# Attention with a relative-position bias and two MLPs on one core: building the bias table with one operand per row, and finishing the last accumulators in turn

## Chip, cores, metric

One core of a Trainium2 chip. The metric is the device time of one execution in microseconds (us). Before the change it is 931.96 us, the median of three runs (929.51 to 933.3).

## The reference

Three stages follow each other. Attention with 4 batches, 8 heads, 576 positions and head size 64 has a bias that depends on the two positions and the head, not on the batch:

```python
psi_rel = np.log1p(np.abs(rel))                    # rel = i - j
psi_i = np.log1p(np.maximum(pos[:, None], 1.0))
x = (psi_rel / psi_i)[..., None]
h = np.maximum(x @ w1 + b1, 0.0)                   # 32 hidden units
bias = h @ w2                                      # [i, j, head]
scores = q @ k.T / sqrt(D) + bias
attn = exp(scores - max) / (sum + 1e-9);  out = attn @ v
```

Two MLPs over 2304 tokens follow: 512 to 1024 to 512 with a softmax gate and a layer norm, then 512 to 2048 to 512 with a piecewise quadratic. All tensors are float32.

## The kernel before

**Bias table (lines 109 to 291).** The table is built once, in DRAM (`bias_d`), and later read back as windows. Its unit of work is u, 16 query positions by all 8 heads; there are 36 units. Partitions hold 4 positions by 32 hidden units, so a unit has four parts c. `emit_r(u)` makes the rows `r[:, c]`: the row `xr` (log of the distance, the same in all partitions) times a column of `sc1` (w1 over psi_i), then a maximum with `kc[:, 0:1]` (minus b1). So a VectorE instruction has two operands that are columns, one value per partition. ScalarE makes c = 0 in four units of five (`on_act`), VectorE the rest. A row has n = `span(u)` = max(576 - 16u, 16u + 16) entries, 304 to 576, since only the distance counts. `emit_c(u)` multiplies them with `w2b` on TensorE into `o` (four column groups of 32). ScalarE then copies `o` twice into `ow`: the left half of the row reversed (line 285) and the right half (line 286), 591 values together, adding a constant `k0`. SyncE's queue writes `ow` to `bias_d` (line 291).

The loop at line 362 emits `emit_r` of one unit and `emit_c` of the unit before. The order of the units is the list `rbs` (line 125), which goes from both ends: 0, 17, 1, 16, 2, 8, and so on. Windows `bt` of the table (`load_bias`, n = 0 to 8; n is two heads by a block of 128 positions, n = 8 the last 64 positions) are loaded as soon as their units are written: n = 8 in round 12, 0 and 1 in round 17, 4 and 5 in round 27, 2 and 3 in round 33; 6 and 7 come behind the loop, and their units are the last ones written. Every fourth round also does one step of `prep_all` (the split of q and k into two parts).

**Attention.** Steps k = 0, 1, ... take one window each: four TensorE matmuls (line 415), one VectorE instruction that adds the bias and takes the maximum (`e`, line 421), ScalarE's exponential (line 436), transposes and the product with v. Weights are split beside it in `step(bw)`.

**Second MLP (lines 891 to 1123).** It runs in five legs of (token half, hidden slices). Each round has seven TensorE groups in the order `SEQ`; between them `GAPS` sets the products with `wo` of the round before. These add to six accumulators `acc` (128 tokens by 512 each). A block (11, 22, 12 or 21) has three units q, one accumulator each; accumulators 0 to 2 take blocks 11 and 21, accumulators 3 to 5 blocks 22 and 12. At a leg's end `evac` copies an accumulator into `ob` (4 buffers) and stores it; in the last two legs it adds a partial sum `pt` that is loaded from `part_d` (3 buffers: three loads ahead, then one more behind each `evac`). `step(bw)` is VectorE work on late weights.

Buffers are handed out in program order, and each engine and DMA queue works strictly in the order in which its instructions are written.

Of the kernel before, what the change touches and what calls it, by code (L numbers as in the profile page):

```python
# [24 lines left out]
KD = DM // 128  # L25
# [13 lines left out]
def tile_attention_moe_moe(  # L39
# [69 lines left out]
    x1 = wa0.tile([2, S], F32, name="x1")  # L109
    one2 = wa0.tile([2, 128], F32, name="one2")  # L110
    xr = wa0.tile([128, S], F32, name="xr")
    sc1 = wa0.tile([128, S // 4], F32, name="sc1")
# [4 lines left out]
    kc = wa0.tile([128, 32], F32, name="kc")  # L117
# [4 lines left out]

    rbs = [0, 17, 1, 16, 2, 8, 3, 9, 4, 10, 5, 11, 6, 12, 7, 13, 14, 15]
# [5 lines left out]
    wz = ps0.tile([128, 512], F32, name="wz")  # L131
# [4 lines left out]
    nc.vector.memset(one2, 1.0)  # L136
    nc.vector.memset(kc[:, 4:5], 0.0)
# [3 lines left out]
    )  # L141
    nc.vector.tensor_tensor(out=dg[:, 0:32], in0=dg[:, 0:32], in1=sml[:, 0:32], op=ALU.mult)
    nc.vector.tensor_reduce(out=dg[:, 32:33], in_=dg[:, 0:32], axis=AX.X, op=ALU.add)
    nc.vector.tensor_scalar(out=kc[:, 0:1], in0=b1c, scalar1=-1.0, scalar2=None, op0=ALU.mult)
    nc.vector.tensor_copy(kc[:, 5:6], b1c)
# [7 lines left out]
    z = ps0.tile([128, 512], F32, name="zs")  # L153

    for c in range(4):
        nc.tensor.matmul(
            z[32 * c:32 * c + 32, 256:258],
            lhsT=flat(w2b),
            rhs=kc[:, 4:6] if c == 0 else b1c.to_broadcast([128, 2]),
            start=True,  # L160
            stop=True,
        )
    nc.vector.tensor_copy(kc[:, 1:3], z[:, 256:258])
    zx = ps0.tile([128, 2, 512], F32, tag="o", name="zx", bufs=3)

    for a in range(4):
        nc.tensor.matmul(
            z[32 * a:32 * a + 32, 0:S // 4],
            lhsT=one2[:, 0:32],
            rhs=x1.rearrange("p (t a) -> p t a", a=4)[:, :, a],  # L170
            start=True,
            stop=True,
        )
    for hf in range(2):
        nc.tensor.matmul(
            zx[:, hf, 0:HS], lhsT=one2, rhs=x1[:, hf * HS:hf * HS + HS], start=True, stop=True
        )
    for _ in range(8):
        nc.tensor.matmul(wz[:, 0:128], lhsT=wt, rhs=wt, start=True, stop=True)
    nc.scalar.copy(out=halves(xr), in_=zx[:, :, 0:HS])  # L180

    nc.vector.reciprocal(out=sc1, in_=z[:, 0:S // 4])
    nc.vector.memset(sc1[0:32, 0:1], 1.0)
    nc.vector.tensor_scalar(out=sc1, in0=sc1, scalar1=dg[:, 32:33], scalar2=None, op0=ALU.mult)
# [63 lines left out]
    r_t = {}  # L248

# [4 lines left out]
    def on_act(u):  # L254
        return u % 5 != 4

    def emit_r(u):
        n = span(u)
        r = wa0.tile([128, 4, S], F32, tag="r", name="r", bufs=3)
        r_t[u] = r  # L260
        for c in range(4):
            w = sc1[:, 4 * u + c:4 * u + c + 1]
            if c == 0 and on_act(u):
                nc.scalar.activation(out=r[:, c, 0:n], in_=xr[:, 0:n], func=ACTF.Relu, scale=w, bias=b1c)  # L264
            else:
                nc.vector.tensor_scalar(
                    out=r[:, c, 0:n], in0=xr[:, 0:n], scalar1=w, scalar2=kc[:, 0:1], op0=ALU.mult, op1=ALU.max
                )

    def emit_c(u):  # L270
        n = span(u)
# [3 lines left out]
        cuts = [0, n] if n <= 512 else [0, 512, n]  # L275
        o = ps0.tile([128, 2, 512], F32, tag="o", name="o", bufs=3)
        for q, (lo, hi) in enumerate(zip(cuts[:-1], cuts[1:])):
            for c in range(4):
                nc.tensor.matmul(  # L279
                    o[32 * c:32 * c + 32, q, 0:hi - lo], lhsT=flat(w2b), rhs=r[:, c, lo:hi], start=True, stop=True  # L280
                )
        o = flat(o)
        k0 = kc[:, 1:2] if on_act(u) else kc[:, 2:3]
# [105 lines left out]
    def ps_s():  # L389
        return ps.tile([128, 2, 512], F32, tag="s", name="ps_s", bufs=2)  # L390
# [806 lines left out]
```

## Time and profile before

| | us |
|---|---|
| median of three runs | 931.96 |
| profiled execution | 931.13 |
| its span, first to last instruction | 929.4 |
| TensorE busy in it | 902.7 (97%) |
| VectorE busy | 721.0 (78%) |
| ScalarE busy | 608.8 (66%) |
| GpSimd busy | 255.4 (27%) |
| chain that ended last: TensorE, VectorE, ScalarE, DMA | 81%, 7%, 5%, 2% |

Times in rows count from the span's start, and the profiled execution takes 1.7 us beyond its span. Engines: PE is TensorE (PEld its weight load), DVE VectorE, ACT ScalarE, POOL GpSimd, SP SyncE; a q behind the name is that engine's queue. A row's duration can reach into the next instruction's start, so what an instruction costs its engine is the distance from its start to the next start; the text calls this the pitch.

### The profile page before, as it was taken

Reading aid. Unit: us, or ns where it says so; the run is one execution under the profiler, and the core shown is the slowest. Engines: PE = TensorE matmul, PEld = TensorE weight load, DVE = VectorE, ACT = ScalarE, POOL = GpSimd, SP = SyncE. Lnnn points to the kernel's source line nnn. Section 1 sums busy time; section 2 is a strip of 40 time slices with the busy share of each in tenths; the row PEclk is TensorE's granted clock in tenths of the full one; section 3 lists DMA queues with packets and bytes.
Section 4 is the critical chain, followed back from the end, with each engine's and each line's share of the span. In section 5 each row is a group of like instructions: output and inputs, shape, how many; then the busy total and the mean of one; then the engine's idle time right before and its main releaser. Section 6 shows DMA issues by size and latency. Waiting matters only on the chain.

```text
span 929.4 us, 16872 instructions
## 1 busy us (share of the span) xinstructions
PE 902.7 (97%) x6052; PEld 778.2 (84%) x6052; DVE 721.0 (78%) x1540; ACT 608.8 (66%) x1290; POOL 255.4 (27%) x229
## 2 busy tenths in 40 slices
PE   8779999999999999999999999999999999999996
PEld 5138888888889889999999998988898888898885
DVE  7997889898888647888888348888888875576854
ACT  5988989999999857666666633555455444454431
POOL 1015665757575324444366400000000000000000
PEclk9999999999999999999999999999999999999998
DMA  4896373564652101555653678769567865347532
GB/s 143 257 298 197 127 253 132 175 222 134 220 167 90 46 23 60 191 193 193 214 206 137 215 260 302 257 203 318 182 228 253 273 210 164 115 159 248 165 119 102
DMA packets 101351, 173.14 MB, mean 186 GB/s; under 512 B 10450, under 2 KB 65234, under 8 KB 101268
## 3 DMA queue, kind: packets, MB, share of 16 engines
q1 hardware_dynamic: 96000, 165.70, 54.3%
q10 hardware_dynamic: 4900, 4.72, 1.4%
q0 software_dynamic: 368, 1.64, 0.5%
q8 instruction: 48, 0.79, 0.3%
q14 instruction: 35, 0.29, 0.1%
HBM read 125.48 MB, written 46.54 MB: 185 GB/s over the span
## 4 chain that ended last, share of the span: by engine, by line
PE 81%; DVE 7%; ACT 5%; DMA 2%; issue 2%; POOL 1%; SPq 0%; DVEq 0%; ACTq 0%
PE acc L1009 20%; PE ab L970 17%; PE ps_s L415 9%; PE ps_x L512 8%; PE ps_s L558 7%; PE ps_t L480 7%; PE ps_x L836 6%; PE ps_s L836 1%; PE o L279 1%; DMA bias_d<-ow 1%; POOL wp L705 1%; PE ps_t L817 1%; PE ps_t L457 1%; PE ps_t L512 1%; ACT r L264 1%
## 5 line engine op out<-in xcount | busy, mean ns | idle before, releaser
L1009 PE MATMUL acc<-wo,gh 128*128 128x512 f32 x576 | 179.4, 392 | 0.2 <-DVE ob L989 0.2
L421 DVE CUSTOM_DVE_ANT_0 e<-ps_s,bt 128x576 f32<-128x576 f32 x144 | 107.7, 749 | 19.8 <-PE ps_s L415 16.5
L1009 PEld LDWEIGHTS acc<-wo,gh 128*128 128x128 f32 x576 | 105.8, 188 | 15.0 <-DVE ob L989 0.8
L436 ACT ACTIVATE e<-e,su 128x576 f32<-128x576 f32 x144 | 112.7, 782 | 8.6 <-DVE su L421 8.1
L1009 PE MATMUL acc<-wo,gl 128*128 128x512 f32 x288 | 114.3, 397 | 0.0
L415 PE MATMUL ps_s<-kh,sq 128*128 128x288 f32 x320 | 101.3, 334 | 3.2 <-DVE su L421 2.8
L956 ACT CAST gh<-ga 128x384 fp32r<-128x384 f32 x96 | 49.4, 514 | 80.5 <-DVE ga L950 80.5
L481 ACT COPY pt<-ps_t 128x512 f32<-128x512 f32 x144 | 83.7, 582 | 11.7 <-PE ps_t L480 9.9
L415 PE MATMUL ps_s<-kl,sq 128*128 128x288 f32 x320 | 89.9, 298 | 0.0
L970 PE MATMUL ab<-x2d,wr 128*128 128x384 f32 x288 | 84.9, 335 | 1.3 <-DVE cs L941 1.3
L945 ACT ACTIVATE ga<-cs,half_c 128x384 f32<-128x384 f32 x72 | 44.4, 616 | 61.2 <-DVE cs L941 61.2
L480 PE MATMUL ps_t<-ident,e 128*128 128x128 f32 x576 | 84.0, 273 | 0.3 <-ACT pt L481 0.3
L957 DVE TENSOR_TENSOR gl<-ga,gh 128x384 fp32r<-128x384 f32 x96 | 53.1, 553 | 33.5 <-ACT gh L956 33.3
L512 PE MATMUL ps_x<-pt,v 128*64 128x256 f32 x640 | 76.2, 384 | 0.0
L936 ACT COPY pk<-ab 128x384 f32<-128x384 f32 x96 | 45.2, 471 | 47.1 <-PE ab L970 46.9
L836 PE MATMUL ps_x<-lh,woh 128*128 128x256 f32 x256 | 73.4, 287 | 0.1
L836 PE MATMUL ps_x<-lh,wol 128*128 128x256 f32 x256 | 72.1, 282 | 0.0
L836 PE MATMUL ps_x<-ll,woh 128*128 128x256 f32 x256 | 72.1, 282 | 0.0
L941 DVE TENSOR_TENSOR cs<-ab,pk 128x384 f32<-128x384 f32 x72 | 39.8, 553 | 40.9 <-PE ab L970 40.9
L480 PEld LDWEIGHTS ps_t<-ident,e 128*128 128x128 f32 x576 | 69.7, 141 | 1.1 <-ACT pt L481 0.5
L415 PEld LDWEIGHTS ps_s<-kh,sq 128*128 128x128 f32 x320 | 61.0, 191 | 11.1 <-DVE sq L217 5.0
L216 POOL TENSOR_TENSOR kl<-stg,kh 128x576 fp32r<-128x576 f32 (+1 forms) x30 | 47.3, 1578 | 67.7 <-DVE kh L213 62.0
(199 smaller groups left out, 2328.5 us busy)
## 6 DMA issues: line engine op xcount, KB each, us to landing
wr<-wi_d SPq DMA_DIRECT2D x168, 256.0 KB, 3.8
stg<-in_qk_dram SPq DMA_DIRECT2D x30, 640.0 KB, 3.9
raw<-in_w2nd_dram SPq DMA_DIRECT2D x32, 512.0 KB, 3.8
wi_d<-wd SPq DMA_DIRECT2D x24, 512.0 KB, 5.6
bias_d<-ow SPq DMA_DIRECT2D x36, 295.5 KB, 3.9
wo_d<-wd SPq DMA_DIRECT2D x16, 512.0 KB, 3.8
wo<-wo_d SPq DMA_DIRECT2D x16, 512.0 KB, 5.5
st<-x_d SPq DMA_DIRECT2D x16, 384.0 KB, 5.5
```

What stands on the lines that cost most here:

```text
L415: nc.tensor.matmul(sc[:, hf, 0:HS], lhsT=l, rhs=r, start=j == 0, stop=j == len(parts) - 1)
L421: nc.vector.tensor_tensor_reduce(out=halves(e), in0=sc[:, :, 0:HS], in1=halves(b_t[hp, n]), scale=-1.0 / float(D) ** 0.5, scalar=3.0e38, o ...
L436: nc.scalar.activation(out=e, in_=e, func=ACTF.Exp, scale=-1.0, bias=su[:, n:n + 1], accum_out=su[:, 9 + n:10 + n])
L480: nc.tensor.transpose(tp[:, kt * 128:(kt + 1) * 128], e[:, c0:c0 + 128], ident)
L481: nc.scalar.copy(out=pt[:, 4 * h:4 * h + 4, 128 * o:128 * o + 128], in_=tp.rearrange("p (a b) -> p a b", a=4))
L512: nc.tensor.matmul(x[64 * h:64 * h + 64, o0:o0 + w], lhsT=v[:, kt, 64 * h:64 * h + 64], rhs=r, start=kt == 0, stop=kt == 4, skip_group_che ...
L558: nc.tensor.matmul(h[:, hf, :], lhsT=l[:, kk, :], rhs=r[:, kk, c0:c0 + 512], start=kk == 0 and j == 0, stop=kk == KD - 1 and j == 2,)
L836: nc.tensor.matmul(ob[:, a * 256:(a + 1) * 256], lhsT=l, rhs=r[:, f, :], start=f == 0 and j == 0, stop=f == K1 - 1 and j == 2,)
L956: nc.scalar.copy(out=gh, in_=a)
L957: nc.vector.tensor_tensor(out=gl, in0=a, in1=gh.bitcast(F32), op=ALU.subtract)
L970: nc.tensor.matmul(d, lhsT=l, rhs=r[:, kk], start=q in (1, 2, 5) and kk == 0 and m == 0, stop=kk == 1 and m == 2, skip_group_check=True,)
L1009: nc.tensor.matmul(d, lhsT=l, rhs=r, start=first and m == 0, stop=last and m == 2, skip_group_check=True)
```

## The change

The bias is written as (xw + sh) with a maximum against zero, summed over the hidden units with w2, and divided by psi_i only when the product is copied. `xw` is the row times w1, `sh` holds b1 times psi_i. A row instruction now has one column operand and an immediate zero. ScalarE makes c = 3 of every unit with bias alone; VectorE always makes three rows. TensorE writes the whole line of 591 values, reading `r` backwards for the left half, in three pieces of four column groups; ScalarE copies it once, times a column of `rs` (1 / psi_i). `rs` comes from a small load `rc0` (64 by 18 single numbers) that GpSimd rounds, a selection matrix `sel` that GpSimd makes, and two TensorE matmuls. The set-up matmuls use the float32r format.

Units go in rising order, `emit_c` follows two rounds behind with four buffers for `r`, and windows 0 to 5 load in pairs in rounds 13, 21 and 29; 6, 7 and 8 follow behind the loop. Step k = 0 of attention moves into round 35 (its exponential into round 36).

In the second MLP all six `pt` are loaded ahead (6 buffers) and the sum is made in place, `ob` has 3 buffers, the first `step(bw)` moves from round 0, q = 7 to round 1, q = 1, and the last round takes its units in the order of `LAST`.

```diff
+    for hf in range(2):
+        nc.tensor.matmul(zx[:, hf, 0:HS], lhsT=one2, rhs=x1[:, hf * HS:hf * HS + HS], start=True, stop=True)
...
+    nc.scalar.activation(out=halves(xw), in_=zx[:, :, 0:HS], func=ACTF.Copy, scale=dg[:, 32:33])
+    nc.vector.tensor_scalar(out=sh, in0=z[:, 0:S // 4], scalar1=b1c, scalar2=None, op0=ALU.mult)
...
+    def emit_rs():
+        nc.gpsimd.tensor_copy(rc, rc0)
+        nc.gpsimd.tensor_tensor(
+            out=sel.rearrange("p o (g e) -> p (o g) e", e=8),
+            in0=ident[0:64, 0:32].unsqueeze(2).to_broadcast([64, 32, 8]),
+            in1=ident[0:64, 32:64].unsqueeze(2).to_broadcast([64, 32, 8]),
+            op=ALU.add,
+        )
+        for o in range(2):
+            nc.tensor.matmul(
+                z[:, 256 + 32 * o:256 + 32 * o + S // 32], lhsT=sel[:, o], rhs=rc, start=True, stop=True
+            )
+        nc.scalar.copy(out=rs.rearrange("p (t o) -> p o t", o=2), in_=...)
...
-    rbs = [0, 17, 1, 16, 2, 8, 3, 9, 4, 10, 5, 11, 6, 12, 7, 13, 14, 15]
+    rbs = list(range(S // 32))
...
     def emit_r(u):
-            w = sc1[:, 4 * u + c:4 * u + c + 1]
-            if c == 0 and on_act(u):
-                nc.scalar.activation(out=r[:, c, 0:n], in_=xr[:, 0:n], func=ACTF.Relu, scale=w, bias=b1c)
+            w = sh[:, 4 * u + c:4 * u + c + 1]
+            if c == 3:
+                nc.scalar.activation(out=r[:, c, 0:n], in_=xw[:, 0:n], func=ACTF.Relu, bias=w)
             else:
                 nc.vector.tensor_scalar(
-                    out=r[:, c, 0:n], in0=xr[:, 0:n], scalar1=w, scalar2=kc[:, 0:1], op0=ALU.mult, op1=ALU.max
+                    out=r[:, c, 0:n], in0=xw[:, 0:n], scalar1=w, scalar2=0.0, op0=ALU.add, op1=ALU.max
                 )
...
     def emit_c(u):
-        nc.scalar.activation(out=ow[:, 0:M - 1], in_=o[:, 1:M][:, ::-1], func=ACTF.Identity, bias=k0)
-        nc.scalar.activation(out=ow[:, M - 1:M - 1 + F], in_=o[:, 0:F], func=ACTF.Identity, bias=k0)
         w = M - 1 + F
+        for lo, hi in ((0, min(M - 1, 512)), (512, M - 1), (M - 1, max(M - 1, 512)), (max(M - 1, 512), w)):
+            if lo < hi:
+                for c in range(4):
+                    d = r[:, c, M - hi:M - lo][:, ::-1] if lo < M - 1 else r[:, c, lo - M + 1:hi - M + 1]
+                    nc.tensor.matmul(o[32 * c:32 * c + 32, lo:hi], lhsT=flat(w2b), rhs=d, start=True, stop=True)
+        nc.scalar.activation(out=ow[:, 0:w], in_=o[:, 0:w], func=ACTF.Copy, scale=rs[:, u:u + 1])
...
     def evac(g, p, k, d):
-        ob = wc.tile([128, DM], F32, tag="ob", name="ob", bufs=4)
+        ob = part_t.pop(0) if g > 2 else wc.tile([128, DM], F32, tag="ob", name="ob", bufs=3)
         if g > 2:
-            nc.vector.tensor_tensor(out=ob, in0=d, in1=part_t.pop(0), op=ALU.add)
-            load_part(p)
+            nc.vector.tensor_tensor(out=ob, in0=d, in1=ob, op=ALU.add)
...
+    LAST = {
+        1: [(22, 0), (22, 1), (22, 2)],
+        2: [(12, 0), (12, 1), (12, 2)],
+        6: [(11, 0), (21, 0), (11, 1), (21, 1), (11, 2), (21, 2)],
+    }
```

**Order on SP's queue around the end of the table, before.** `bt` is a window (the heads of a pair in one or three pieces), `raw` a piece of the first weights; the last three windows' places are at issue.

```order
L291 DMA bias_d<-ow 16x8x591 x12
L240 DMA bt<-bias_d 64x576 x2
...
L291 DMA bias_d<-ow 16x8x591 x3
L345 DMA raw<-in_win_dram 128x256 x2
L242 DMA bt<-bias_d 128x576
L244 DMA bt<-bias_d 128x512
L245 DMA bt<-bias_d 128x64
L201 DMA v<-in_vp_dram 128x640
```

And with the change:

```order
L299 DMA bias_d<-ow 16x8x591
L258 DMA bt<-bias_d 128x576
L260 DMA bt<-bias_d 128x512
L261 DMA bt<-bias_d 128x64
L299 DMA bias_d<-ow 16x8x591 x8
L353 DMA raw<-in_win_dram 128x256 x2
L258 DMA bt<-bias_d 128x576
L260 DMA bt<-bias_d 128x512
L261 DMA bt<-bias_d 128x64
L256 DMA bt<-bias_d 64x576 x2
L217 DMA v<-in_vp_dram 128x640
```

Window 8 (the piece of 64 positions, twice) moves from the first third of the table to behind windows 6 and 7; what stands between the last write and window 6 is the same.

**Order on ACT at the table's start, before**, from the copy of the row on (`r` a row, `ow` a copied half):

```order
L180 ACTIVATE xr<-zx 128x576
L264 ACTIVATE r<-xr,sml,sc_95 128x576
L264 ACTIVATE r<-xr,sml,sc_95 128x560
L285 ACTIVATE ow<-o,kc 128x15
L286 ACTIVATE ow<-o,kc 128x576
L285 ACTIVATE ow<-o,kc 128x31
L286 ACTIVATE ow<-o,kc 128x560
```

And with the change:

```order
L170 ACTIVATE xw<-zx,dg 128x576
L278 ACTIVATE r<-xw,sh 128x576
L194 COPY rs<-zz 128x2x18
L278 ACTIVATE r<-xw,sh 128x560
L278 ACTIVATE r<-xw,sh 128x544
L295 ACTIVATE ow<-o,rs 128x591
L278 ACTIVATE r<-xw,sh 128x528
L295 ACTIVATE ow<-o,rs 128x591
```

The copy of `rs` stands behind the first row, and every unit has one row and one copy on this engine.

**Order on PE at the very end, before** (accumulators 0 to 5 are 6943, 6944, 6945, 6946, 6949, 6950; gh and gl the two parts of a block; from the fourth unit of the last round on):

```order
L1009 MATMUL acc_6946<-wo_9322,gh 128x512 x2
L1009 MATMUL acc_6946<-wo_9322,gl 128x512
...
L1009 MATMUL acc_6946<-wo_9174,gh 128x512 x2
L1009 MATMUL acc_6946<-wo_9174,gl 128x512
...
L1009 MATMUL acc_6943<-wo_9322,gh 128x512 x2
L1009 MATMUL acc_6943<-wo_9322,gl 128x512
```

And with the change (accumulators 3 and 0 are 7173 and 7170, from the fourth unit of the last round on):

```order
L1019 MATMUL acc_7173<-wo_9401,gh 128x512 x2
L1019 MATMUL acc_7173<-wo_9401,gl 128x512
...
L1019 MATMUL acc_7170<-wo_9401,gh 128x512 x2
L1019 MATMUL acc_7170<-wo_9401,gl 128x512
L1019 MATMUL acc_7170<-wo_9549,gh 128x512 x2
L1019 MATMUL acc_7170<-wo_9549,gl 128x512
```

Block 12 comes three units earlier, and an accumulator of the first three is finished every two units instead of every unit at the very end.

## Rows read from the trace of the kernel before

**Rows 1.** Windows: us, busy us per engine, PE clock, DMA share, GB/s.

```profile
16.00:64.00 48.00, 36.29 (x308) 10.44 (x308) 46.03 (x109) 44.54 (x95) 0.00 (x0) 1.00 0.86 267
80.00:100.00 20.00, 20.00 (x183) 17.10 (x180) 17.26 (x48) 17.20 (x45) 12.89 (x12) 1.00 0.37 116
```

**Rows 2.** Timeline, set-up and first units: start us, us, instruction, idle before.

```profile
1.06 3.78 PE L133 MATMUL wz<-wt 128*128 128x128 f32 x16 [1.06 <-DVE half_c L127]
...
8.98 7.81 DVE L266 TENSOR_SCALAR r<-xr,sc,kc 128x576 f32<-128x576 f32 x16 [1.35 <-ACT xr L180]
...
11.91 3.35 PE L279 MATMUL o<-r,w2b 128*32 128x512 f32 x48
...
14.38 15.12 SPq L291 DMA_DIRECT2D bias_d<-ow  x11
```

**Rows 3.** Groups by form on DVE: busy us, mean ns.

```profile
L266 DVE TENSOR_SCALAR r<-xr,sc,kc 128x576 f32<-128x576 f32 x6 | 3.1, 574 | 1.4 <-ACT xr L180 1.4
...
L266 DVE TENSOR_SCALAR r<-xr,sc,kc 128x304 f32<-128x304 f32 x6 | 2.3, 433 | 0.0
...
L213 DVE CAST kh<-stg 128x576 fp32r<-128x576 f32 x2 | 0.9, 452 | 0.0
...
L184 DVE TENSOR_SCALAR sc<-sc,dg 128x144 f32<-128x144 f32 x1 | 0.3, 296 | 0.0
```

**Rows 4.** Timeline of ACT and DVE, early units, the last rows and the last copy.

```profile
14.57 0.72 ACT L286 ACTIVATE ow<-o,kc 128x560 f32<-128x560 f32 x1
15.18 0.86 ACT L264 ACTIVATE r<-xr,sml,sc 128x576 f32<-128x576 f32 x1
15.94 0.72 ACT L285 ACTIVATE ow<-o,kc 128x559 f32<-128x559 f32 x1
16.55 0.29 ACT L286 ACTIVATE ow<-o,kc 128x32 f32<-128x32 f32 x1
...
60.71 1.45 DVE L266 TENSOR_SCALAR r<-xr,sc,kc 128x512 f32<-128x512 f32 x3
...
63.99 0.32 ACT L286 ACTIVATE ow<-o,kc 128x80 f32<-128x80 f32 x1
```

**Rows 5.** Groups by form on ACT, first 75 us.

```profile
L436 ACT ACTIVATE e<-e,su 128x576 f32<-128x576 f32 x7 | 5.4, 774 | 3.6 <-DVE su L421 3.5
```

**Rows 6.** Chain of waits, table into attention: start us, us, what.

```profile
65.41 4.70 DMA bias_d<-ow
...
70.25 2.81 DMA bt<-bias_d
...
73.19 0.76 DVE e L421
...
74.01 2.29 PE ps_s L415 x8
```

**Rows 7.** Windows behind that wait, columns as in rows 1.

```profile
74.00:76.00 2.00, 1.99 (x8) 1.99 (x9) 1.56 (x5) 2.00 (x5) 0.00 (x0) 0.50 0.98 333
```

**Rows 8.** Timeline of PE, first round of the second MLP.

```profile
551.36 0.45 PE L970 MATMUL ab<-x2d,wr 128*128 128x384 f32 x1 [0.68 <-DVE cs L941]
```

**Rows 9.** Timeline of PE, ACT and DVE at the end.

```profile
915.25 0.62 PE L1009 MATMUL acc<-wo,gh 128*128 128x512 f32 x2
...
921.14 0.39 PE L1009 MATMUL acc<-wo,gl 128*128 128x512 f32 x1
...
915.78 1.22 DVE L957 TENSOR_TENSOR gl<-ga,gh 128x384 fp32r<-128x384 f32 x2
...
921.89 0.69 DVE L989 TENSOR_TENSOR ob<-acc,pt 128x512 f32<-128x512 f32 x1 [1.67 <-DMA out_dram<-ob]
...
925.40 0.69 DVE L989 TENSOR_TENSOR ob<-acc,pt 128x512 f32<-128x512 f32 x1 [0.63 <-DMA pt<-part_d]
...
914.84 0.51 ACT L956 CAST gh<-ga 128x384 fp32r<-128x384 f32 x1 [0.21 <-DVE ga L950]
```

**Rows 10.** Chain of waits at the end.

```profile
920.80 4.48 DMA pt<-part_d
```

More of the change, by code (lines that the diff above doesn't have):

```diff
@@ L116, in tile_attention_moe_moe @@
     w2b = wa0.tile([128, 4, 8], F32, name="w2b")
[L117 removed]
     XR = (S // 32) * S
[L122 removed]
+    nc.scalar.dma_start(
+        out=x0, in_=bass.AP(xcon.tensor, xcon.offset + XR, [[32 * XR, 2], [1, S]])
+    )
     nc.sync.dma_start(out=sml, in_=small)
[L125 removed]
+    nc.sync.dma_start(
+        out=rc0, in_=bass.AP(xcon.tensor, xcon.offset + 1, [[XR, 64], [S, S // 32], [1, 1]])
+    )
+    nc.vector.memset(one2.bitcast(F32), 1.0)
+    nc.vector.memset(onea.bitcast(F32), 0.0)
+    for a in range(4):
+        nc.vector.memset(onea[:, a, 32 * a:32 * a + 32].bitcast(F32), 1.0)
     nc.vector.memset(wt, 0.0)
@@ L152, in tile_attention_moe_moe @@
     )
[L153 to L161, printed above, removed]
-        )
[L163 to L172, printed above, removed]
-        )
[L174 to L184, printed above, removed]
+    def emit_rs():
[5 more added lines that the diff above has]
+            op=ALU.add,
+        )
+        for o in range(2):
+            nc.tensor.matmul(
+                z[:, 256 + 32 * o:256 + 32 * o + S // 32], lhsT=sel[:, o], rhs=rc, start=True, stop=True
+            )
+        nc.scalar.copy(
+            out=rs.rearrange("p (t o) -> p o t", o=2),
+            in_=z[:, 256:320].rearrange("p (o t) -> p o t", o=2)[:, :, 0:S // 32],
+        )
+    rbs = list(range(S // 32))
+    EB, LT, LP = 4, 5, 7
     kh_t, kl_t, sq_t, v_t, stg_t = {}, {}, {}, {}, {}
@@ L438, in emit_exp, with ps_s, ps_t, ps_x @@
         )
+    bg = prep_all()
+    first = {35: 0}
+    us = [2 * rb + o for rb in rbs for o in range(2)]
+    for p in range(NB + 2):
+        if p == 0:
+            load_qk(0, nc.gpsimd)
+            load_qk(1, nc.gpsimd)
+            load_v(0, nc.gpsimd)
+        if p < NB:
+            emit_r(us[p])
+        if p == 0:
+            emit_rs()
+        if p > 1:
+            emit_c(us[p - 2])
+        if p in first:
+            emit_qk(first[p], ps0.tile([128, 2, 512], F32, tag="zz", name="zz", bufs=1))
+        elif p - 1 in first:
+            emit_exp(first[p - 1])
+        for n in {13: (0, 1), 21: (2, 3), 29: (4, 5)}.get(p, ()):
+            load_bias(0, n)
+        if p % 4 == 0 and 4 <= p <= 32:
+            step(bg)
+    bw = split_w(list(range(32)), load_w1)
+    for n in (6, 7, 8):
+        load_bias(0, n)
+    es_p0.close()
+    es_a0.close()
+    es_w1, w1pool = opened(pool("w1p"))
+    wih = w1pool.tile([128, KD, F1], F32R, name="wih")
+    wil = w1pool.tile([128, KD, F1], F32R, name="wil")
+    woh = w1pool.tile([128, K1, DM], F32R, name="woh")
+    wol = w1pool.tile([128, K1, DM], F32R, name="wol")
+    es_p, ps = opened(pool("ps1", space=PS))
+    def ps_s():
+        return ps.tile([128, 2, 512], F32, tag="s", name="ps_s", bufs=2)
+    def ps_t():
+        return ps.tile([128, 512], F32, tag="t", name="ps_t", bufs=3)
+    def ps_x():
+        return ps.tile([128, 512], F32, tag="x", name="ps_x", bufs=1)
     def emit_norm(u, c):
@@ L618, in tile_attention_moe_moe @@
             if c == "Q":
-                emit_qk(k)
+                if k not in first.values():
+                    emit_qk(k)
                 if b == B - 1 and hp + 1 < HP:
@@ L624, in tile_attention_moe_moe @@
             elif c == "E":
-                emit_exp(k)
+                if k not in first.values():
+                    emit_exp(k)
             elif c == "P" and 0 <= k - LP < NK:
@@ L1061, in tile_attention_moe_moe @@
             parts.extend((3, 4, 5, 0, 1, 2))
-            for _ in range(3):
+            for _ in range(6):
                 load_part(p)
@@ L1074, in tile_attention_moe_moe @@
                 load_wo(n)
+                if n == 1:
+                    step(bw)
             elif q == 2:
@@ L1099, in tile_attention_moe_moe @@
                 relu((n, 22))
-                if conv(n):
+                if n > 0 and conv(n):
                     step(bw)
```

94 lines of the change are left out of this document (34 added, 60 removed).

## Prediction

> **What bounds the kernel now.** The windows come first. From 80 us on TensorE is busy without a break [rows 1], so whatever brings the first attention step forward reaches the end. In the 48 us of the table before that, VectorE works 46.0 and ScalarE 44.5 us, TensorE only 36.3, and the DMA engines are busy 0.86 of the time at 267 GB/s [rows 1]. The table is thus bound by VectorE and ScalarE together, with DMA not far behind. The timeline gives its edges: the first rows start at 8.98, the first group of products at 11.91, the first write is issued at 14.38 [rows 2], the last copy ends at 63.99 + 0.32 = 64.31 [rows 4]. The chain of waits shows the join with attention: last write, load of a window, `e` at 73.19, TensorE at 74.01 [rows 6], and behind it TensorE runs 2 us at a granted clock of 0.50 [rows 7]. At the end, the chain shows TensorE stopping at 921.53 while the sums go on to 926.09 [rows 9], held by a load of `pt` [rows 10]. These are the three places that the change touches.
>
> **The change part by part.** The sum is made against the profiled execution, 931.13 us (0.8 below the median of 931.96, inside its runs).
>
> *Row instructions on VectorE.* Sixteen of the first take 7.81 us, 0.49 each, which is the 574 ns of the group less 0.085 of overlap; 576 entries against 304 give 0.52 ns per entry [rows 2, 3]. By that line an instruction with two columns would take 574 - 432 x 0.52 = 350 ns at 144 entries; the one-operand instruction of 144 took 296. I take 54 ns for the second operand. The ends are 0 and the 122 ns by which the cast, with no column, lies below the row at the same 576 [rows 3]. 108 rows remain, 36 units of three: 108 x 0.054 = 5.8 us, and the 7 that go to ScalarE give 7 x 0.42 (at the mean of 440 entries) = 2.9. From 8.98 to the end of the last rows, 60.71 + 1.45, VectorE is busy 53.2 us [rows 2, 4]; it now needs some 44.5.
>
> *ScalarE.* It had per unit a row (0.76 from start to start at 576) and two copies (0.61 for 559 reversed, 0.61 for 560 forward) [rows 4]. Now it has one row and one copy of 591. The exponential, with bias alone, takes 774 ns at 576 where the row takes 860 [rows 4, 5], so a row with bias alone costs 0.67 at 576 and, by the copies' slope of about 1 ns per entry, 0.55 at the mean of 440. The copy comes to 0.61 x 591/560 = 0.64. That is 1.19 us a unit.
>
> *TensorE* took 3.35 us for the first three units, 1,696 columns [rows 2], 1.97 ns each. 591 columns give 1.17 us a unit: nearly ScalarE's figure. That holds if a reversed column costs what a forward one does; 10,620 of the 21,276 are reversed. No row has TensorE reading backwards. The nearest is ScalarE, whose 559 reversed take the same 0.72 as 560 forward [rows 4]. I take no extra; the ends are none and one column time again, 1.97 ns.
>
> *The start.* The set-up matmuls in float32r and the dropped casts let the first rows start near 6.2 instead of 8.98. Then the second warm-up, as long as the first (3.78 [rows 2]), and the two matmuls for `rs` come before the first product. I put that at 9.5 instead of 11.91 (between 8.5 and 13), the first unit's end at 9.5 + 1.17 = 10.7 and the first write at 11.8.
>
> *End of the table.* Behind 10.7, ScalarE has 33 rows at 0.55, 36 copies at 0.64 and the first exponential: 18.2 + 23.0 + 0.7 = 41.9. At the share it has now, 44.54 of 48 or 0.93, that takes 45.1 and ends at 55.8, say **56** (54.3 without idle after the first units, 57.5 if all three engines wait on each other more often). **Gain 64.3 - 56 = 8.3 us** (6.8 to 10).
>
> *The join.* Now the first step waits for a last write of 4.70 and then a load of 2.81 [rows 6]. With the change windows 0 to 5 are loaded long before, six steps are ready, and step 0 runs inside the last rounds; only windows 6 to 8 need the last writes, and step 0 and its followers cover 7 us. TensorE begins behind the last product, some 3 us sooner relative to the last copy, and it doesn't come out of a pause; the 2 us at half clock cost 1 us now [rows 7]. But casts of the weights, moved against it, and the loads of v in a queue already at 0.98 of its time [rows 7] take some of it back. I take **2.7 us** (0 to 4.5).
>
> *Moved weight step.* TensorE waits 0.68 in the second MLP's first round for `cs`, behind `step(bw)` on VectorE [rows 8]. In round 1 that work stands beside rounds where TensorE is never short: **0.7 us** (0 to 0.7). If its new place were short, the same 0.68 would come back there.
>
> *The tail.* All `pt` are present, so the last sum follows the last product directly. But block 12 comes three units earlier, at 915.25, when its gh is ready only at 914.84 + 0.51 = 915.35, and its gl around 916.4 (two instructions from 915.78) [rows 9]. TensorE has one unit of 0.6 to fill that, so it loses about 0.7 and stops at 922.2. The sum ends 0.7 later (0.69 [rows 9]) at 922.9 rather than 926.09: **3.2 us** (1.5 to 3.9).
>
> *Three `ob` for four.* In legs 0 to 2 each group of three evacuations may wait for a store; the wait at 921.89 was 1.67 [rows 9]. Products of the next leg hide most of it: **-0.4 us** (0 to -1.7).
>
> Sum: 8.3 + 2.7 + 0.7 + 3.2 - 0.4 = 14.5, and 931.13 - 14.5 = **916.6 us**.
>
> **Rivals.**
> *DMA paces the table.* 0.86 of 48 us for 267 x 48 = 12.8 MB [rows 1] is 310 GB/s of busy time. By the end of the table 14.0 MB must now pass: 36 writes of 303 KB (128 x 591 x 4 bytes), six windows of 295 KB (128 x 576 x 4), 1.3 MB of q and k. That is 45.1 us behind the first write at 11.8, so 56.9, and 58.5 with the delay of a last write whose `ow` buffer is waited for. For it: DMA is the only resource that the change does not make cheaper. Against: the queue also moves before the first write. Time 916.6 + 2.5 = 919.1, with a little lost at the join 919.6.
>
> *A second column operand costs VectorE nothing.* Then it needs 53.2 - 2.9 = 50.3 us from 6.2, two units follow, and the last copy ends near 58.8: 919.4. For it: the 296 ns of one instruction are thin evidence. [...] The rows speak against it: at the same 576 entries the cast and the row differ by 122 ns [rows 3].
>
> *GpSimd comes late.* `sel` and `rc` stand ahead of the first product on TensorE. In 16 to 64 us GpSimd did nothing at all [rows 1], so no row shows it beside row instructions; if it only gets through when VectorE pauses, with its four `r` buffers full at about 11.4, and needs 1.6 us then, the first product starts at 13.0 instead of 9.5, and the end moves by 3.5: 920.1. [...] Against it: in 80 to 100 us the two are busy 17.26 and 12.89 of 20 [rows 1], more than 20 together, though with other instructions.
>
> *Reversed reading on TensorE is slow.* This is the one that ends slower. At twice the price per reversed column, 10,620 x 1.97 ns = 20.9 us come on TensorE, which then paces the table: 916.6 + 20.9 = 937.5. The gain of 14.5 is gone at 14.5/10,620 = 1.4 ns extra per reversed column. For it: no row shows it. Against: ScalarE's 559 and 560 [rows 4].
>
> **How the numbers follow.** My forecast, ScalarE in step with TensorE at 916.6, 0.53. DMA 919.6, 0.20. GpSimd 920.1, 0.12. Operand 919.4, 0.10. Reversed 937.5, 0.05. The likeliest case's own range is 912 to 921 (table 6.8 to 10, join 0 to 4.5, tail 1.5 to 3.9, not all at one end). A half per cent, 4.7 us, is about what a measurement can tell from no change, so faster is below 927.3 and slower above 936.6. The first four cases lie below 927.3 unless two of them and a lost join come together (0.04 of it). So faster 0.91, same 0.05, slower 0.04. The range goes down to 910.5 with every term at its good end, and up to 924.5, which is GpSimd late or DMA with no gain at the join.
>
> **What would show it.** Right, step by step: a row of 576 on VectorE from start to start near 0.44; one row and one copy on ScalarE in 1.19 us; first products near 9.5 and the first write near 11.8; the last copy near 56; TensorE without a pause between table and attention and no stretch at 0.50 there; no 0.68 before `ab` in the second MLP's first round; the last sum within a microsecond of the last product, some 3.3 us before the end. Wrong: DMA near 1.0 with ScalarE waiting for `ow` (DMA); 0.49 on VectorE (operand); the first product after 12 with TensorE waiting on GpSimd; more than 1.5 us for a unit of 12 products on TensorE (reversed). A whole forecast is wrong if the last copy ends before 56 but the time stays above 925: then the earlier start was taken back behind 80 us, by the changed order of windows or in the second MLP.

## The result, and the profile after

The changed kernel takes 919.89 us (median of 4 runs, 919.48 to 921.8), the kernel before 930.74 in the same comparison: a ratio of 0.9886, with a 95% interval of 0.9863 to 0.9908. The forecast of 916.6 was 3.3 us too low, and the time lies in the range and on the side that was given. The span of the profiled execution went from 929.4 to 918.3 us, by 11.1; the forecast had 14.5.

The windows of the table and behind it (columns as in [rows 1]), in the changed kernel; the last row is its whole stretch from the first write to the last copy:

```profile
14.00:32.00 18.00, 17.47 (x354) 12.69 (x347) 17.94 (x51) 16.97 (x29) 0.00 (x0) 1.00 0.82 238
32.00:56.00 24.00, 24.00 (x465) 13.86 (x456) 23.07 (x61) 22.27 (x37) 0.69 (x1) 1.00 0.99 333
56.00:60.00 4.00, 1.31 (x26) 1.05 (x16) 0.77 (x2) 2.57 (x5) 2.44 (x2) 1.00 0.91 321
60.00:72.00 12.00, 9.61 (x63) 9.04 (x62) 7.96 (x23) 8.27 (x22) 3.77 (x3) 0.86 0.94 298
...
13.40:59.60 46.20, 43.02 (x836) 27.70 (x828) 42.37 (x114) 42.01 (x71) 3.13 (x2) 1.00 0.90 292
```

And 32 to 56 us in the kernel before:

```profile
32.00:56.00 24.00, 17.64 (x140) 4.86 (x136) 23.93 (x61) 22.30 (x48) 0.00 (x0) 1.00 0.93 290
```

VectorE is still busy nearly all of the time, as it was, and the DMA engines are at 0.99 from 32 to 56 us, where they had 0.93 before. TensorE's busy time has risen to the whole stretch, but the ends of its products are modelled, and their starts show room: units 14 to 17, whose rows are ready, begin at 29.06, 30.07, 31.07 and 32.08, 1.00 us apart, while VectorE's rows come at one unit in 1.2 us (43.7 us for 36). From 56 to 60 the three compute engines are idle for a third of the time or more, while DMA goes on.

The set-up and first units, in the timeline of the changed kernel (answers to [rows 2]):

```profile
6.36 0.70 PE L161 MATMUL zz<-x,onea 2*128 2x144 f32 x4
6.57 0.74 ACT L170 ACTIVATE xw<-zx,dg 128x576 f32<-128x576 f32 x1 [3.75 <-PE zx L157]
6.82 0.62 POOL L184 TENSOR_TENSOR sel<-ident 64x256 fp32r<-64x256 f32 x1
6.99 2.05 PE L169 MATMUL zz<-wt 128*128 128x128 f32 x16
9.08 0.37 DVE L172 TENSOR_SCALAR sh<-zz,sml 128x144 f32<-128x144 f32 x1 [6.07 <-PE zz L169]
9.85 6.28 DVE L280 TENSOR_SCALAR r<-xw,sh 128x576 f32<-128x576 f32 x15
...
13.39 3.04 SPq L299 DMA_DIRECT2D bias_d<-ow  x3
```

The products that `sh` needs (L161) are done at 7.06, but `sh` is read at 9.08, behind the second warm-up (L169), which writes the other half of the same PSUM tile `zz`. So the first row starts at 9.85, later than before [rows 2], though GpSimd is done at 7.44.

VectorE's rows by form (answers to [rows 3]):

```profile
L280 DVE TENSOR_SCALAR r<-xw,sh 128x576 f32<-128x576 f32 x6 | 2.7, 514 | 0.0
L280 DVE TENSOR_SCALAR r<-xw,sh 128x304 f32<-128x304 f32 x6 | 1.8, 375 | 0.0
```

574 became 514 ns and 433 became 375. The 108 rows and the preparation between them run from 9.85 to 53.59, 43.7 us, where 115 rows and the preparation took 53.2. The end of the table on ScalarE (timeline), and this engine's waits up to 70 us (in total, times, longest):

```profile
54.83 0.76 ACT L295 ACTIVATE ow<-o,rs 128x591 f32<-128x591 f32 x1 [0.15 <-DMA bias_d<-ow]
57.43 0.76 ACT L295 ACTIVATE ow<-o,rs 128x591 f32<-128x591 f32 x1 [1.84 <-DMA bias_d<-ow]
...
58.84 0.74 ACT L295 ACTIVATE ow<-o,rs 128x591 f32<-128x591 f32 x1
```

```profile
ACT ow L295 <- DMA bias_d<-ow: 3.1, 4, 1.8
ACT ow L295 <- PE o L294: 1.9, 3, 0.9
```

The last rows are done at 53.59, the last products at 56.22, and yet the last copy ends at 58.84 + 0.74 = 59.58: it waits for an `ow` buffer whose write has not landed. The join, in the chain of waits (answers to [rows 6]):

```profile
51.12 6.23 DMA bias_d<-ow
57.43 0.56 ACT ow L295
...
59.61 0.52 SPq L299
60.18 0.58 SPq L353
60.81 0.44 SPq L353
61.35 6.28 DMA bt<-bias_d
67.76 0.76 DVE e L390
68.58 1.33 PE ps_s L384 x8
```

The load of window 6 takes 6.28 us where it took 2.81 [rows 6]. Before that, TensorE has a pause of another cause, in its timeline: the scores of step 2 need PSUM space that the late copies still hold.

```profile
59.63 0.40 PE L384 MATMUL ps_s<-kh,sq 128*128 128x288 f32 x1 [2.69 <-ACT ow L295]
```

Behind this pause its clock falls again (windows of 2 us; answers to [rows 7]):

```profile
60.00:62.00 2.00, 1.67 (x11) 1.44 (x10) 1.53 (x5) 1.07 (x4) 0.00 (x0) 0.75 0.86 247
62.00:64.00 2.00, 2.00 (x10) 1.99 (x10) 1.47 (x4) 1.44 (x5) 1.55 (x1) 0.50 0.98 222
```

The end of the second MLP (timeline; answers to [rows 9]). The wait of 0.26 shown is for the early block 12, and the last sum stands directly behind the last product:

```profile
908.41 0.51 PE L1019 MATMUL acc<-wo,gl 128*128 128x512 f32 x1 [0.26 <-DVE gl L968]
...
914.00 0.39 PE L1019 MATMUL acc<-wo,gl 128*128 128x512 f32 x1
```

```profile
914.42 0.69 DVE L1000 TENSOR_TENSOR pt<-acc,pt 128x512 f32<-128x512 f32 x1 [0.67 <-PE acc L1019]
```

Where the 11.1 us come from can be read by laying the same instruction of both traces side by side. The last copy comes 64.31 - 59.58 = 4.7 us earlier. From attention step k = 14 to the start of the second MLP everything is 6.85 earlier, so the join gave 2.1. One hundred `ab` products later it is 7.87 (542.93 to 572.76 before, 536.10 to 564.89 after): 1.0 from the moved weight step. The last `ab` product ends 7.97 earlier; the tail from there to the end of the span went from 16.0 to 12.9 us: 3.1. About 0.1 lies in the rounds between.

### The profile page after: what moved, and what is told of

Same layout as the page of the kernel before. It is cut to its first block, busy times and chain, and to the rows that moved or that the text cites. A ratio compares the mean times of both kernels' runs of the same rounds, so it can differ in the third digit from the quotient of the medians.

```text
span 918.3 us, 17872 instructions
## 1 busy us (share of the span) xinstructions
PE 904.4 (98%) x6552; PEld 792.8 (86%) x6552; DVE 710.6 (77%) x1534; ACT 604.2 (66%) x1262; POOL 256.0 (28%) x231
## 4 chain that ended last, share of the span: by engine, by line
PE 82%; DVE 8%; ACT 4%; issue 2%; DMA 2%; POOL 1%; SPq 0%; DVEq 0%; ACTq 0%
PE acc L1019 20%; PE ab L981 18%; PE ps_s L384 9%; PE ps_x L522 8%; PE ps_t L490 7%; PE ps_s L568 6%; PE ps_x L847 4%; PE o L294 3%; PE ps_s L847 1%; DMA bias_d<-ow 1%; POOL wp L716 1%; DVE wp L713 1%; PE ps_t L467 1%; PE ps_t L522 1%; DVE wp L705 1%
## 5 line engine op out<-in xcount | busy, mean ns | idle before, releaser
L968 DVE TENSOR_TENSOR gl<-ga,gh 128x384 fp32r<-128x384 f32 x96 | 53.2, 554 | 34.2 <-ACT gh L967 34.0
L1019 PEld LDWEIGHTS acc<-wo,gl 128*128 128x128 f32 x288 | 54.0, 187 | 12.4 <-DVE gl L968 1.0
```

Of the source, the lines that this page charges most:

```text
L968: nc.vector.tensor_tensor(out=gl, in0=a, in1=gh.bitcast(F32), op=ALU.subtract)
L1019: nc.tensor.matmul(d, lhsT=l, rhs=r, start=first and m == 0, stop=last and m == 2, skip_group_check=True)
```

## The experiments

Times of spans are those of profiled executions; the changed kernel's is 918.3. One caution holds for all: the program up to the second MLP is the same in the changed kernel, in "second MLP as before" and in "old order in the last round", and yet e of step k = 8 starts at 70.11, 68.77 and 70.38. So the join varies by 1.6 us by itself, and a single span shows no less than that. Ahead of the join the last row repeats within 0.1 us in these three (53.53 to 53.59), but the last copy ends at 59.58, 59.14 and 60.26, so it varies by 1.1. The kernel before, run beside four groups of these runs, has medians from 929.95 to 931.83 us.

### Second MLP as before

```diff
-            nc.vector.tensor_tensor(out=ob, in0=d, in1=ob, op=ALU.add)
+            nc.vector.tensor_tensor(out=ob, in0=d, in1=part_t.pop(0), op=ALU.add)
+            load_part(p)
...
-                if n == 1:
-                    step(bw)
...
-            for blk, u in (GAPS if n < NS else LAST).get(q, ()):
+            for blk, u in GAPS.get(q, ()):
```

> The second MLP as before, the table and attention as changed. Theory: the two traces put 6.85 us of the gain ahead of the attention steps' steady state and the other 4.25 us (11.1 - 6.85) behind it, so the span is 918.3 + 4.25 = 922.5 us, TensorE waits 0.68 for cs again, and the span ends about 7.9 us after the last product instead of 3.9. Rival: the second MLP only absorbs what comes before it (its loads set its end); then this run loses less than 2 us, span below 920.3.

Measured: span 920.9, median 924.59. Its join happened to come 1.4 earlier; from the first `ab` product on it takes 920.93 - 534.62 = 386.3 us, the changed kernel 918.30 - 536.10 = 382.2. So the second MLP's edits give 4.1 us by themselves, as the theory said: 1.0 by the moved step (29.81 instead of 28.79 us for the first hundred `ab` products) and 3.1 at the tail.

### Old order in the last round

```diff
-            for blk, u in (GAPS if n < NS else LAST).get(q, ()):
+            for blk, u in GAPS.get(q, ()):
```

> All partial sums are loaded ahead and summed in place, as changed, but the last round takes its units in the old order, so the last three accumulators are finished one unit (0.68 us) apart at the very end. Theory (the loads of the partial sums were what held the end, as the prediction has it): a sum of 0.69 us keeps up with a unit of 0.68, TensorE does not wait 0.26 for gl, and the span is 918.3 within 0.5. Rival (finishing the accumulators in turn is what pays): sums and stores bunch at the end, the span ends 5 us or more behind the last product instead of 3.9, span 919.3 to 920.5.

Measured: span 917.4, median 919.69. The end, in this run's timeline of VectorE: all six sums in one piece.

```profile
910.10 4.09 DVE L1000 TENSOR_TENSOR pt<-acc,pt 128x512 f32<-128x512 f32 x6 [1.17 <-PE acc L1019]
```

A sum of 0.69 us keeps up with a unit of 0.68, so finishing the accumulators in turn buys nothing. It costs: from the last `ab` product to its own end TensorE needs 9.02 us in the changed kernel, 8.20 here and 8.20 before. From the last `ab` product to the end of the span it is 12.9 us in the changed kernel and 12.2 here. The gain of the tail is that of the partial sums loaded ahead and summed in place; before, the sums waited 1.67 us for an `ob` buffer and then for a load [rows 9], and no run separates the two.

### Two columns in a row instruction

```diff
-                    out=r[:, c, 0:n], in0=xw[:, 0:n], scalar1=w, scalar2=0.0, op0=ALU.add, op1=ALU.max
+                    out=r[:, c, 0:n], in0=xw[:, 0:n], scalar1=w, scalar2=zc, op0=ALU.add, op1=ALU.max
```

> The maximum takes a column of zeros instead of the immediate zero, so a row instruction has two columns again. Theory (a column operand costs 54 ns, and VectorE paces the table): the row of 576 goes from 514 to about 570 ns, the 108 rows take 43.7 + 5.8 = 49.5 us, and the end moves by 4 to 6 us, span 922 to 924. Rival (the operand is free, rows got cheaper for another reason): 514 ns stays and the span stays at 918.3 within 1. Rival (DMA paces the table's end): the row gets longer, but the span moves by less than 3 us.

Measured: span 924.0, median 925.53. The rows by form, where `zc` is the column of zeros:

```profile
L282 DVE TENSOR_SCALAR r<-xw,sh,zc 128x304 f32<-128x304 f32 x6 | 2.2, 432 | 0.0
L282 DVE TENSOR_SCALAR r<-xw,sh,zc 128x576 f32<-128x576 f32 x3 | 1.6, 573 | 0.0
```

The second column costs 573 - 514 = 59 ns at 576 entries and 432 - 375 = 57 at 304: a price per instruction. The rows take 50.3 us instead of 43.7. They also start 2.0 later in this run, because its second warm-up ran long (`sh` at 11.06), so they end 8.5 later; the last copy ends only 64.53 - 59.58 = 5.0 later. The difference is what DMA had been behind the rows: here ScalarE waits for `ow` 0.7 us in all, not 3.1. So the operand's price is shown, and that VectorE alone does not set the end of the table in the changed kernel. How much of the span's 5.7 us is the operand's and how much the later start's, this run does not separate.

### Warm-up in a tile of its own

```diff
-    z, wz = zz[:, 0], zz[:, 1]
+    z, wz = zz[:, 0], ps0.tile([128, 2, 512], F32, tag="o", name="wz", bufs=3)[:, 0]
```

> The warm-up products go to a PSUM tile of their own, so that VectorE's sh does not wait for the second warm-up. Theory (that wait is what made the rows start late, and VectorE paces the table from its first row on): sh starts near 7.2 instead of 9.08, the first row near 7.9 instead of 9.85, and the whole chain comes 1.9 us forward, span 916.4. Rival (the DMA engines pace the end of the table): the first write comes 1.9 us earlier, the last copy less than 1 us earlier, span 917.3 to 918.3. Rival (GpSimd shut out by VectorE's rows): sel, at 6.82 to 7.44 before the first row now, is done in time in any case, no effect.

Measured: span 917.5, median 919.26. The set-up of this run, in the timeline, and ScalarE's wait:

```profile
6.00 0.69 PE L161 MATMUL zz<-x,onea 2*128 2x144 f32 x4
6.72 0.37 DVE L172 TENSOR_SCALAR sh<-zz,sml 128x144 f32<-128x144 f32 x1 [3.59 <-PE zz L161]
...
7.70 6.27 DVE L280 TENSOR_SCALAR r<-xw,sh 128x576 f32<-128x576 f32 x15
```

```profile
ACT ow L295 <- DMA bias_d<-ow: 4.0, 3, 2.1
```

The wait for the second warm-up is the shared tile's: without it the rows start 2.15 us earlier and end 2.16 earlier, the last products end 2.55 earlier. The last copy comes only 1.24 earlier, little more than the 1.1 by which it varies, and ScalarE waits more for `ow`. That is between the two expectations: part of the earlier start is lost again to the wait for writes. The span's 0.8 is within the join's own variation, and the time can't be told from the changed kernel's.

### More DMA load

```diff
+        if p in (10, 15, 18, 23, 26, 31):
+            xd = wa0.tile([128, 400], F32, tag="xd", name="xd", bufs=1)
+            nc.sync.dma_start(out=xd, in_=qk[3, 7][:, 0:400])
```

> Six loads of 205 KB that nobody reads are put on SP's queue in rounds 10 to 31, 1.23 MB, 4.0 us at the 310 GB/s of busy time. Theory (the DMA engines pace the table's end, since they were busy 0.9 to 1.0 of the time from 32 us on): the last copy comes 2 to 4 us later, ScalarE waits longer for ow (3.1 us now), span 920.3 to 922.3. Rival (VectorE's rows pace the table, the wait at the end is only the latency of a write): last copy within 1 us, span within 1 us of 918.3.

Measured: span 922.8, median 924.53. The waits of ScalarE, a wait of SP's queue, and windows of this run:

```profile
ACT ow L295 <- DMA bias_d<-ow: 6.8, 5, 1.9
```

```profile
SPq L429 <- DMA xd<-in_qk_dram: 2.9, 2, 2.2
```

```profile
32.00:56.00 24.00, 20.77 (x390) 12.19 (x382) 21.59 (x57) 18.71 (x33) 0.00 (x0) 1.00 0.92 291
...
60.00:72.00 12.00, 8.19 (x59) 7.67 (x49) 4.64 (x12) 8.06 (x18) 5.43 (x4) 0.72 0.96 317
...
36.00:40.00 4.00, 2.82 (x48) 1.74 (x52) 3.62 (x10) 2.42 (x5) 0.00 (x0) 1.00 0.71 241
```

And 36 to 40 us in the changed kernel:

```profile
36.00:40.00 4.00, 4.00 (x88) 2.75 (x81) 4.00 (x12) 3.95 (x8) 0.00 (x0) 1.00 0.97 327
```

The last copy ends at 64.70, 5.1 us later, more than the 4.0 that the bytes would take; the span is 4.5 longer. Now VectorE has gaps too (21.59 of 24, 23.07 in the changed kernel), presumably because `ow`, then `o`, then `r` come free late (the author's reading, not shown). But the edit does more than add bytes. The six loads share one buffer (`bufs=1`), so SP's queue stands 2.9 us in all until an earlier one has landed, with the writes of the table behind it, and in such a stretch the DMA engines are less busy, not more (36 to 40 us). So the run shows that the end of the table hangs on this queue and its transfers, and not on VectorE's rows alone; how much of the 5.1 us is bytes, it does not separate. The cleaner test is "head 3 late" below, with 655 KB less: the rows end at 53.59 as they did, and the last copy comes 1.75 earlier, at 57.83, where the three runs that are alike there lie between 59.14 and 60.26. More `ow` buffers, which might spare ScalarE that wait, were not tried.

### Mirrored half by ScalarE

```diff
-                    d = r[:, c, M - hi:M - lo][:, ::-1] if lo < M - 1 else r[:, c, lo - M + 1:hi - M + 1]
-                    nc.tensor.matmul(o[32 * c:32 * c + 32, lo:hi], lhsT=flat(w2b), rhs=d, start=True, stop=True)
-        nc.scalar.activation(out=ow[:, 0:w], in_=o[:, 0:w], func=ACTF.Copy, scale=rs[:, u:u + 1])
+        nc.scalar.activation(out=ow[:, 0:M - 1], in_=o[:, 1:M][:, ::-1], func=ACTF.Copy, scale=rs[:, u:u + 1])
+        nc.scalar.activation(out=ow[:, M - 1:w], in_=o[:, 0:F], func=ACTF.Copy, scale=rs[:, u:u + 1])
```

> The mirrored half goes back to ScalarE: TensorE writes the row once, and ScalarE copies it in two parts, the left one reversed. Theory (the single copy matters because ScalarE would pace the table otherwise): ScalarE takes 0.55 + 0.78 = 1.33 us a unit instead of 1.2, 48 us for the 36 units, the last copy near 61 to 62, span 919.5 to 921. Rival (VectorE and DMA pace the table, ScalarE has room, and TensorE is relieved): last copy within 1 of 59.5, span within 1 us of 918.3.

Measured: span 918.5, median 921.5. The table of this run:

```profile
16.00:56.00 40.00, 38.40 (x266) 11.34 (x264) 37.66 (x103) 40.00 (x92) 0.00 (x0) 1.00 0.91 295
```

ScalarE is now full (40.00 of 40), as the theory said, and its waits for `ow` are all but gone; but the last copy ends at 60.19, 0.6 later and within its own variation, and the span is the same. By the profile, the mirrored half on TensorE bought next to nothing here: ScalarE with two copies arrives when DMA does.

### Left half read forwards

```diff
-                    d = r[:, c, M - hi:M - lo][:, ::-1] if lo < M - 1 else r[:, c, lo - M + 1:hi - M + 1]
+                    d = r[:, c, M - hi:M - lo] if lo < M - 1 else r[:, c, lo - M + 1:hi - M + 1]
```

> The left half is read forwards too; the output then has a mirrored left half of the bias and is not the reference's. Theory (a reversed column costs TensorE what a forward one does): four units take the same 4.95 us back to back (1.24 a unit) and the span stays at 918.3 within 0.5. Rival (reversed reading has a price): a unit falls from 1.24 us towards 1.17, some 2.5 us over 36 units, with TensorE waiting for rows instead.

Measured: span 918.9, median 922.11. TensorE's groups by form between 18 and 56 us for two widths that only left halves have, first the changed kernel (reversed), then this run (forwards):

```profile
L294 PE MATMUL o<-r,w2b 128*32 128x399 f32 x8 | 1.3, 510 | 0.0
...
L294 PE MATMUL o<-r,w2b 128*32 128x495 f32 x8 | 1.4, 590 | 0.0
```

```profile
L294 PE MATMUL o<-r,w2b 128*32 128x399 f32 x8 | 1.3, 510 | 0.0
...
L294 PE MATMUL o<-r,w2b 128*32 128x495 f32 x8 | 1.4, 590 | 0.0
```

To the nanosecond the same. Since ends of products are modelled, the starts say more, and they agree: in this run units 15 to 18 begin at 29.44, 30.45, 31.46 and 32.47, as far apart as units 14 to 17 of the changed kernel (29.06 to 32.08). A reversed column has no price on TensorE here. The rival that ended slower had no ground. The four first units, which the expectation named, can't be compared: in this run they fell into a stretch at a lower clock, shown in the last section.

### Three ways to reorder DMA

Windows ahead of the raw weights:

```diff
-    bw = split_w(list(range(32)), load_w1)
     for n in (6, 7, 8):
         load_bias(0, n)
+    bw = split_w(list(range(32)), load_w1)
```

> The loads of windows 6, 7 and 8 are issued before the first two loads of raw weights instead of behind them. Theory (the chain from the last copy over the window's load holds the step k = 6, and the two raw loads, 1.17 us on SP's queue and 0.5 MB, lie in it): e of k = 6 at about 66.3 instead of 67.76, attention 1.2 to 2.5 us earlier, span 916 to 917. Rival (the DMA engines pace everything, and the weights are then missed): e moves, but TensorE or VectorE waits for raw or its split later, span 918 to 919.

Windows 6 and 7 before the last write:

```diff
-        for n in {13: (0, 1), 21: (2, 3), 29: (4, 5)}.get(p, ()):
+        for n in {13: (0, 1), 21: (2, 3), 29: (4, 5), 36: (6, 7)}.get(p, ()):
...
-    for n in (6, 7, 8):
-        load_bias(0, n)
+    load_bias(0, 8)
```

> Windows 6 and 7 need units 24 to 31 only; here they are loaded in round 36, before the last unit's write, and only window 8 waits for it. Theory (the join is bound by the wait for the last writes): e of k = 6 comes 2 to 3 us sooner, window 8 (two steps later) becomes the wait, span 915.5 to 917. Rival (SP's queue stands in that wait for the write of unit 31, and the last writes go out later; the same bytes pass in any case): the last copy moves to 60 or later, span 918 to 919.5.

Head 3 behind the windows (its casts at steps 7 and 8):

```diff
-            load_qk(s + 2)
+            if s != 1:
+                load_qk(s + 2)
...
     for n in (6, 7, 8):
         load_bias(0, n)
+    load_qk(3)
...
+    late = {4: "QTWE", 5: "QPpRET", 7: "BBBQTWE", 8: "SNBBQTE"}
...
-        for c in order[n] if k < NK else tail.get(n, "TP"):
+        for c in late.get(k, order[n]) if k < NK else tail.get(n, "TP"):
```

> The load of head 3's q and k (655 KB, 2.1 us at 310 GB/s) leaves the table and goes behind the windows; its casts go from steps 4 and 5 to steps 7 and 8. Theory (DMA paces the table's end): ScalarE's 3.1 us of waiting for ow shrinks to about 1, the last copy comes about 2 us earlier (57.5 instead of 59.5), span 916 to 917. Rival (what is moved is paid behind the windows): e of k = 8 and the steps behind it stay where they are, or step 10 waits for head 3, span 918 or more.

| | last copy ends | e, k = 6 | e, k = 8 | e, k = 20 | span | median |
|---|---|---|---|---|---|---|
| changed kernel | 59.58 | 67.76 | 70.11 | 91.83 | 918.3 | 919.89 |
| windows first | 59.59 | 65.11 | 70.17 | 91.89 | 918.2 | 921.16 |
| 6 and 7 early | 61.02 | 66.62 | 70.37 | 91.81 | 918.6 | 920.65 |
| head 3 late | 57.83 | 65.79 | 70.60 | 94.41 | 921.5 | 922.4 |

Each moved the wait that it aimed at, and step 8 stayed within half a microsecond: the rivals were right three times. With the windows first, window 6 is there 2.65 us earlier, but the first weights are then missed: their split on VectorE stands between steps 6 and 7 and waits, which holds steps 7 and 8.

```profile
68.49 0.30 DVE L321 TENSOR_SCALAR wp<-raw 128x256 uint32<-128x256 uint32 x1 [2.63 <-DMA raw<-in_win_dram]
```

With 6 and 7 early, the last copy is 1.4 later. With head 3 late, the last copy is 1.75 earlier, and the load is missed behind the join, where VectorE and the scores wait:

```profile
69.11 0.49 DVE L229 CAST kh<-stg 128x640 fp32r<-128x640 f32 x1 [1.56 <-DMA stg<-in_qk_dram]
```

That cast stands ahead of step 7. By step 8 the run is 0.5 us behind the changed kernel, by step 20 2.6; the rest of the span's 3.2 comes in the second MLP, whose stretch from the first to the last `ab` product varies by as much between runs that are alike there (368.6 to 369.7 us). The loads that VectorE needs up to step 8 are the same in all four kernels, and that step comes at nearly the same time; this agrees with their sum setting it, but no run shows it by itself.

### The two together, and with the old order

The edits of "head 3 late" and "warm-up in a tile of its own", and then the old order of the last round as well.

> Head 3's load late and the warm-up in a PSUM tile of its own. Theory (rows on VectorE and the DMA engines pace the table together, so that only both moved bring the full gain): rows end at 51.4, the last copy near 55.5 to 56.5, span 914.8 to 916 where the two alone gave 917.5 and what the run beside this one gives. Rival (the windows' loads hold the join whatever comes before): span within 0.5 of the better of the two alone.

> As the run before it, and the last round takes its units in the old order. Theory: as measured alone (TensorE 9.02 us from the last ab product to its end against 8.20), another 0.8 us, span 914 to 915.2. Rival: that difference was chance, span as in the run before it.

Measured: spans 921.8 and 918.5, medians 922.83 and 921.74. Up to the last copy the gains add: rows end at 51.7 and 51.6, the last copies at 56.26 and 55.98, 3.3 and 3.6 us before the changed kernel's. But step 20 comes at 95.25 and 93.09, later than 91.83: head 3 is waited for as above (3.5 us on VectorE in the first, 1.7 in the second). Between the two, the end on TensorE again takes 9.01 and 8.20 us, the 0.8 of the old order; the rest of their difference is the join's. Neither beats the changed kernel. The warm-up apart with the old order, but without moving head 3, was not run.

## Why the prediction was right, and where it was not

**Operand: right.** 54 ns were taken, 57 to 59 measured; VectorE's rows took 43.7 us where 44.5 were forecast. The rival that it costs nothing falls: with the column of zeros the same rows take those 57 to 59 ns more.

**ScalarE: right in size, but not the pace. TensorE: put too high.** A row of ScalarE takes 0.56 us from start to start at 448 entries and 0.66 at 560, a copy 0.64, as forecast. A unit on TensorE was put at 1.17 us; where the rows are ready it takes 1.00, and it was not the partner in step with ScalarE that the forecast made of it. (The first four units take 4.95 us, 1.24 each, but VectorE's rows come no faster there: 15 in 6.28 us, 1.26 for the three of a unit.)

**The start: wrong.** The first rows were put at 6.2 and came at 9.85, the first write at 11.8 and came at 13.39. The step missed that `z` and the warm-up share a tile, so that `sh` stands behind the warm-up; the experiment with a tile of its own shows 2.15 us of it; the other 1.5 of the first row stay open. GpSimd, the rival's suspect, was done at 7.44, before the first row, so the runs do not show it beside row instructions at the start. No run shows the 1.6 us either that the rival gave it: `rc` and `sel` took 0.78 us here (6.66 to 7.44).

**The end of the table: the step that failed.** It let ScalarE set the end at its present share of 0.93 and came to 56; the last copy ended at 59.58, and so 3.6 us of gain are missing here (4.7 instead of 8.3). The other terms together give 0.2 back, which makes the 3.4 between 14.5 forecast and 11.1 measured. The runs put two things in the place of ScalarE's share: the late start and the DMA transfers. With the rows 2.15 earlier the last copy came 1.24 earlier; with 655 KB moved out of the table it came 1.75 earlier; with both it ended at 56.26 and 55.98, the 56 of the forecast. ScalarE does not decide: with two copies a unit it was full, and the last copy moved by 0.6, which is within its variation. The DMA rival came closest in its mechanism, with 45.1 us of transfers behind the first write; with that write at 13.39 it is 58.5. That this lies 1.1 from the 59.58 is in part luck: the engines were not busy all of that time, but 0.90 of it, and moved 324 GB/s while busy (292 / 0.90), not 310. So is that the rival's own time, 919.6, is 0.3 from the median: its first write was 1.6 too early.

**The join: 2.1 instead of 2.7, a difference inside its own variation.** In "second MLP as before" and "old order in the last round", with the same table and attention, the last copy comes 5.2 and 4.1 earlier than before the change and the join gives 3.1 and 2.8. No run isolates what in the join gives it. The steps 0 to 5 do cover much of the last writes: their `e` start at 54.09 to 63.62, the last write goes out at 59.61, and window 6 is there at 61.35 + 6.28 = 67.63. But the text expected no pause and no stretch at half clock, and both are there: the scores of step 2 wait for a PSUM buffer that the late copies still hold, and the clock is 0.75 and 0.50 behind that pause.

**Moved weight step: 1.0 instead of 0.7.** The wait of 0.68 [rows 8] is gone, and a little more.

**Tail: 3.1 instead of 3.2, with the parts as said.** TensorE loses 0.8 by the early block 12 (0.7 said), and the sums no longer wait for a load [rows 10]. The old order shows that the gain was to be had without that loss.

**Three `ob` for four: nothing seen instead of 0.4.** ScalarE now waits four times for a buffer whose store has not landed, in the legs of the second MLP, which it did not before; no wait of TensorE stands behind them (waits of ScalarE from 536 us on):

```profile
ACT ob L1002 <- DMA out_dram<-ob: 1.5, 2, 1.0
...
ACT ob L1002 <- DMA part_d<-ob: 1.0, 2, 0.5
```

## What to carry to other kernels

Where several engines and the DMA queues are nearly full in one stage, work out for each when it would be done, DMA by its bytes over the rate that the trace shows while it is busy, and take the latest: cheaper instructions moved the end of this stage by 4.7 us where 8.3 were forecast, because the first write came late and the transfers then lasted longer than the rows. Before a load is moved past the point that it blocks, look for where it lands and when it is needed: with head 3 late the last copy came 1.75 us earlier, but a cast then waited 1.56 us for the load, in a stretch where DMA was busy 0.94 of the time already (60 to 72 us in the changed kernel), and step 20 came 2.6 us later. And in this kernel `sh`, whose products were done at 7.06, was read only at 9.08, when the warm-up in the other half of their tile was done, and at 6.72, 0.03 behind its products, where the warm-up had a tile of its own; so look for what else writes to a tile before a start is dated.

## What was not expected of the hardware

The set-up varies from run to run in its second warm-up. With the same 16 products, the first row starts at 9.85 in the changed kernel and at 11.83 with two columns, where TensorE, busy all of 5 to 8 us in both, did 13 products in it against 19. The granted clock reads 1.00 there in both. In the run with the left half forwards the first units, right behind the set-up, run at a granted clock of 0.60 although TensorE is busy all of 12 to 16 us, where the changed kernel has 1.00; "windows first", which is the changed kernel up to there, has 0.60 as well, so the reading order is not the cause:

```profile
12.00:16.00 4.00, 4.00 (x56) 1.88 (x60) 4.00 (x11) 2.97 (x5) 0.00 (x0) 0.60 0.30 80
```

What decides it stays open. The join, too, varies by 1.6 us between identical programs, with the same bytes queued.
